# Re-ordering the first loads, the bound chain and the plan of layer 1's first stage in a two-layer linear-attention / gated-MLP kernel

## The chip, the cores and the metric

The kernel runs on one core of a Trainium2 chip. The metric is the device time of one launch in microseconds (us), the median of several runs. In what follows PE is the matrix engine, DVE the vector engine, ACT the scalar engine, POOL the GpSimd engine, and SP the engine that issues most DMA transfers; ACT issues a few of its own.

## The reference, cut to what matters

Four residual steps on `x` of 2048 tokens by 576, in bf16: attention A, MLP B, attention A, MLP B, all with the same weights.

```python
def A(x):                                  # 32 heads of 18
    q, k, v = split(layernorm(x) @ wqkv)   # wqkv: 576 x 1728
    pq, pk = q @ w_phi, k @ w_phi          # w_phi: per head 18 x 18
    phi_q = concat(softmax(pq), softmax(-pq))
    phi_k = concat(softmax(pk), softmax(-pk))
    kv, z = phi_k.T @ v, phi_k.sum(over tokens)
    return (phi_q @ kv) / (phi_q @ z + 1e-6) @ wo
def B(x):
    n = layernorm(x)
    return ((n @ w_gate) * (n @ w_up)) @ w_down     # 576 -> 4608 -> 576
x = x + A(x); x = x + B(x); x = x + A(x); x = x + B(x)
```

`kv` and `z` sum over all tokens, so no token of a layer gets its attention output before the key side of all tokens is done. This is the barrier of each layer.

## The kernel before, in words

The 2048 tokens are 16 tiles of 128 tokens, in 8 pairs ("blocks"). The model width of 576 is cut into five slices of 128 rows, the last one holding 64 rows twice. `w_phi` is multiplied into the query and key weights at the start, so that `x @ Wk` gives `pk` at once: `t_fuse1` (L1003) takes one row block of the raw weights (`Wraw`, five blocks), transposes its five 128-column pieces on PE (L1012), copies them from PSUM to `WT` (L1015), multiplies by a block-diagonal `w_phi` (`BDphi`, L879 and L1025), and copies the result into `Wk` or `Wq` (L1031).

The program has two versions of everything behind a branch: softmax without the subtraction of a maximum ("fast"), taken if a bound shows that no exponent can overflow, and a general one. The bound is worked out by `t_flag` (L883). It needs the largest entry of `w_phi` (L888), the diagonal blocks of `Wraw`'s Gram matrix, summed over all five row blocks (L893, fifty 128x128 matmuls), the row maxima of these on DVE (L896), a transposition of three columns on PE in f32 (L901), and four small DVE steps in a row (L907 to L910), the last of which writes the flag. Each engine loads the flag and branches (L248, L249). What stands ahead of the branch in each engine's program is the shared part. In these runs the fast version is taken.

The first stage after the branch is layer 1's key side. For each tile, layer norm (`t_ln`, L1042) does bn_stats twice (L1066), an aggregate (L1074), the reciprocal root on ACT (L1087, L1089), and the normalised tile `xln` on POOL or DVE (L1099, a piece of 576 columns, and a repeat of 64 for tiles that a DMA transposes). The tile is transposed by PE (L1107, L1110) for the first four tiles and by a DMA (L1114) for the rest. `t_v` (L1346) projects values (PE L1140, ACT copies L1370). `t_ain` with `fast_front` projects keys (PE L1140, four ACT exponentials L1261), and `softmax_tail` sums (DVE L1327), inverts (ACT L1334, or DVE L1330) and multiplies (L1342: POOL, or DVE for the last two tiles). `kv_ops` accumulates `kv` in two PSUM banks (PE L1381). Key tiles use six buffers, which come free when `kv_ops` has read them. A projection here is 18 matmuls on row halves of 64.

`t_qproj` (L1271) projects queries of tiles 2 to 15 and stores them in place of the tile (PE L1140, ACT L1284). `t_aout` (L1475) turns a tile's queries into its attention output. For tiles 0 and 1 of layer 1 it does so by PE transposes (L1493), and only after the barrier (`t_barrier`, the masked copy `BD`, L1466) come the numerator (L1523), its division (L1531 to L1545), the output projection (L1557, L1578, L1128) and the second layer norm. Then the MLP of block 0 starts (`gu_quad`, PE L1662). From there on, MLP blocks (gate and up L1662, down L1736 and L1738) run back to back, with the attention work of later tiles laid between their matmuls.

Nothing of this order is written by hand. Each `t_` function is a thread of a planner (`Sched`, L295 on), which at build time estimates when each operation could start and appends the earliest to its engine's program, corrected by priorities, by per-thread constants in `AGES` (L19), and by per-operation costs. Each engine then runs its list in order, waiting on semaphores. So a change in a cost, a priority or an age moves instructions throughout; on the chip an instruction that waits holds up all that stand behind it on its engine.

The loads at the start (`t_load`, L915): SP issues tile 0 of x, raw block 0, raw block 2, tile 1, raw block 4 (64 rows, loaded twice into the two partition halves), the value weights `Wv` in three transfers, and tiles 2 to 7 in three. ACT issues `w_phi` in two, raw block 1 and raw block 3.

## Time and profile before

| what | value |
|---|---|
| median of 6 runs | 1078.48 us (1077.53 to 1079.17) |
| the profiled execution's own time | 1078.44 us |
| its span in the trace | 1076.7 us |
| PE busy | 1053.4 us, 98% |
| DVE, ACT, POOL busy | 483.7, 346.1, 202.2 us |
| first bound matmul (L893) | 4.20 us |
| flag written (end of L910) | 19.14 us |
| first sum of exponentials (L1327) | 27.40 us |
| `BD` done (L1466) | 84.50 us |
| first matmul of the MLP (L1662) | 101.32 us |

Times in the trace count from the start of the span. The span is 1.74 us shorter than the execution's time, which lies around it. "PE busy" counts a matmul from its start to its modelled end, so PE that waits a little inside a group still counts as busy.

### The profile page before, as it was taken

The page shows a single profiled execution, that of the slowest core. Times are in us where ns is not written, and L with a number is a line of the kernel's source. Part 1 is how long each engine was busy: PE and PEld are TensorE (multiplying, and loading weights), DVE is VectorE, ACT ScalarE, POOL GpSimd, SP SyncE. Part 2 cuts the span into 40 slices and gives each one's busy share as a digit, 9 for nine tenths or more (in the row PEclk, how much of TensorE's full clock was granted, in tenths as well). Part 3 has the DMA queues.
Part 4 walks back from the last instruction along what each step waited for, and adds up shares of the span by engine and source line. Part 5 has one row for each costly group of instructions (what it writes and reads, how often), then busy time and mean ns, then how long its engine had stood idle before and what let it go on. Part 6 is the DMA issues. An engine that isn't in the chain of part 4 may idle for free.

```text
span 1076.7 us, 34366 instructions
## 1 busy us (share of the span) xinstructions
PE 1053.4 (98%) x15812; PEld 806.9 (75%) x15812; DVE 483.7 (45%) x974; ACT 346.1 (32%) x838; POOL 202.2 (19%) x232
## 2 busy tenths in 40 slices
PE   6999999999999999999999999999999999999997
PEld 5667868778686878878685787777778686868683
DVE  5986436344443535425332754434434243424131
ACT  4777224314241422314140642231313131302120
POOL 2764004022130403103020030201010101000000
PEclk9999999999999999999999999999999999999999
DMA  4486264260916335181605134536271809080604
GB/s 134 113 271 239 38 187 85 71 177 14 225 35 194 65 113 140 38 194 37 199 14 166 35 58 113 146 87 171 63 196 39 220 19 239 15 222 16 210 2 146
DMA packets 177642, 127.79 MB, mean 119 GB/s; under 512 B 96592, under 2 KB 175696, under 8 KB 176336
## 3 DMA queue, kind: packets, MB, share of 16 engines
q1 hardware_dynamic: 176592, 124.85, 44.5%
q8 instruction: 126, 2.06, 0.8%
q10 hardware_dynamic: 896, 0.64, 0.2%
q14 instruction: 28, 0.23, 0.1%
HBM read 100.82 MB, written 2.36 MB: 96 GB/s over the span
## 4 chain that ended last, share of the span: by engine, by line
PE 92%; DMA 2%; POOL 2%; DVE 2%; ACT 1%; issue 0%; ACTq 0%
PE ps L1662 53%; PE ps L1736 22%; PE ps L1140 11%; PE ps L1738 3%; PE ps L1523 1%; DMA wdx<-in_B_w_down_dram 1%; POOL dd_w3f L1342 1%; PE ps L1381 1%; PE ps L1128 1%; DMA Wraw<-in_A_wqkv_dram 1%; DVE xln L1099 1%; POOL dd_h1g L1342 1%; DVE ss_w4f L1327 0%; DMA wdr<-in_B_w_down_dram 0%; PE ps L1107 0%; PE ps L893 0%
## 5 line engine op out<-in xcount | busy, mean ns | idle before, releaser
L1662 PE MATMUL ps<-xT,Wg 64*128 64x256 bf16 x4608 | 582.3, 269 | 0.0
L1662 PE MATMUL ps<-xT,Wu 64*128 64x256 bf16 x4608 | 582.0, 269 | 0.0
L1662 PEld LDWEIGHTS ps<-xT,Wu 64*128 64x128 bf16 x4608 | 432.1, 94 | 27.4 <-DVE x_sb L1777 0.3
L1662 PEld LDWEIGHTS ps<-xT,Wg 64*128 64x128 bf16 x4608 | 430.7, 94 | 28.8 <-issue 3.1
L1711 DVE TENSOR_TENSOR hT<-ps,hT 128x512 bf16<-128x512 f32 x288 | 199.2, 692 | 299.8 <-ACT hT L1709 299.8
L1709 ACT CAST hT<-ps 128x512 bf16<-128x512 f32 x288 | 168.4, 585 | 412.2 <-PE ps L1662 402.2
L1736 PE MATMUL ps<-wdr,hT 128*128 128x512 bf16 x960 | 244.2, 380 | 1.3 <-DMA wdr<-in_B_w_down_dram 1.3
L1342 POOL TENSOR_TENSOR dd<-dd,ss 128x576 bf16<-128x576 bf16 x92 | 107.5, 1194 | 415.4 <-ACT ss L1338 415.4
L1738 PE MATMUL ps<-wdr,hT 128*128 128x64 bf16 x960 | 185.1, 193 | 0.0
L1736 PEld LDWEIGHTS ps<-wdr,hT 128*128 128x128 bf16 x960 | 93.8, 98 | 112.4 <-DMA wdr<-in_B_w_down_dram 1.9
L1662 PE MATMUL ps<-xT,Wr 64*128 64x256 bf16 x1152 | 170.4, 269 | 0.0
L1099 POOL TENSOR_SCALAR xln<-x_sb,nmean,rstd 128x64 bf16<-128x64 bf16 (+1 forms) x94 | 58.2, 625 | 340.1 <-DVE nmean L1080 157.9
L1779 DVE TENSOR_TENSOR x_sb<-ps,x_sb 128x64 bf16<-128x64 f32 x32 | 7.1, 221 | 224.8 <-PE ps L1738 224.8
L1738 PEld LDWEIGHTS ps<-wdr,hT 128*128 128x128 bf16 x960 | 94.1, 98 | 0.2
L1338 ACT ACTIVATE ss<-ss 128x64 f32<-128x64 f32 x92 | 23.6, 258 | 175.8 <-DVE ss L1327 175.0
L1327 DVE TENSOR_REDUCE ss<-dd 128x64 f32<-128x1152 bf16 x48 | 63.8, 1348 | 21.1 <-ACT dd L1261 16.1
L1662 PEld LDWEIGHTS ps<-xT,Wr 64*128 64x128 bf16 x1152 | 66.8, 94 | 6.2
L1736 PE MATMUL ps<-wdx,hT 128*128 128x512 bf16 x192 | 54.3, 380 | 1.2 <-DMA wdx<-in_B_w_down_dram 1.1
L1140 PE MATMUL ps<-Wk,xT 64*128 64x288 bf16 x576 | 49.9, 286 | 2.3 <-ACT vx_w0g L1370 1.4
L1140 PE MATMUL ps<-Wv,xT 64*128 64x288 bf16 x576 | 49.1, 288 | 0.0
L1066 DVE BATCH_NORM_STATS2 st<-x_sb 128x6 f32<-128x288 bf16 x120 | 46.3, 445 | 2.3 <-DMA x_sb<-in_A_x_dram 1.5
L1140 PE MATMUL ps<-Wo,oT 64*128 64x288 bf16 x504 | 40.5, 283 | 0.0
(120 smaller groups left out, 741.4 us busy)
## 6 DMA issues: line engine op xcount, KB each, us to landing
wdr<-in_B_w_down_dram SPq DMA_DIRECT2D x240, 288.0 KB, 3.6
wdx<-in_B_w_down_dram SPq DMA_DIRECT2D x48, 288.0 KB, 3.7
Wg<-in_B_w_gate_dram SPq DMA_DIRECT2D x4, 1152.0 KB, 14.9
Wu<-in_B_w_up_dram SPq DMA_DIRECT2D x4, 1152.0 KB, 16.9
out_dram<-x_sb SPq DMA_DIRECT2D x16, 144.0 KB, 2.3
x_sb<-in_A_x_dram SPq DMA_DIRECT2D x7, 288.0 KB, 5.3
xT<-xln SPq DMA_TRANSPOSE x54, 2.6
Wraw<-in_A_wqkv_dram SPq DMA_DIRECT2D x2, 304.0 KB, 4.1
```

The source lines that it names most:

```text
L1066: ops.append(Op(d_dve(288), (lambda e, j=j, h=h, src=src: e.bn_stats(st[:, sl[j], 6 * h:6 * h + 6], src)), reads=rd, writes=[("st", sl[j], ...
L1099: em = [(lambda e, j=j, a=a, b=b, c=c: e.tensor_scalar(xln[:, sl[j], a:b], x_sb[:, ss[j], c:c + b - a], s.nmean[:, sl[j]:sl[j] + 1], rstd[ ...
L1128: full = [Op(d_pe(N), (lambda e, k=k, h=h: e.matmul(s.ps[:, banks[h], 0:N], L[:, k, :], Wm[:, k, N * h:N * h + N], start=(k == 0 and fresh ...
L1140: out.append(Op(61, (lambda e, h=h, k=k, st=(i == 0 and k == 0), sp=(i == 1 and k == 3): e.matmul(s.ps[:, banks[h], 0:N], L[r, k, :], Wm[r ...
L1327: Op(1265, (lambda e: e.tensor_reduce(ss[:, sm, :], e4, AX.X, ALU.add)), reads=s.ddk(sm, 0) + s.ddk(sm, 1), writes=[("ss", sm)]),
L1338: yield ("ops", "act", [Op(200, (lambda e, kw=kw: e.activation(ss[:, sm, :], ss[:, sm, :], **kw)), reads=[("ss", sm)], writes=[("ss", sm)])])
L1342: yield ("alt", [(eng, [Op(dur, (lambda e, ev=ev, rb=rb: e.tensor_tensor(ev, ev, rb, ALU.mult)), reads=s.ddk(sm, br) + [("ss", sm)], write ...
L1662: out.append(Op(54.3, (lambda e, bank=bank, cs=cs, lhsT=lhsT, rhs=rhs, st=st, sp=sp: e.matmul(ps[:, bank, cs].rearrange("p (a n) -> p a n" ...
L1709: yield ("ops", "act", [Op(480, (lambda e, gb=gb, p=p: e.copy(hT[:, p, :], ps[:, gb, :])), reads=[("gu", gb)], writes=[("hT", p)] + (s.raw ...
L1711: yield ("ops", "dve", [Op(600, (lambda e, ub=ub, p=p: e.tensor_tensor(hT[:, p, :], ps[:, ub, :], hT[:, p, :], ALU.mult)), reads=[("gu", u ...
L1736: ops = [Op(d_pe(512), (lambda e: e.matmul(s.ps[:, bank, 0:512], lhsT, s.wslot(slot)[:, fi, 0:512], start=(f == 0), stop=(f == NF - 1))), ...
L1738: Op(d_pe(64) + 3, (lambda e: e.matmul(s.ps[:, z, 64 * sl:64 * sl + 64], lhsT, s.wslot(slot)[:, fi, 512:576], start=(f == 0 and (sl == 0 o ...
```

## The change

It has these parts.

1. Loads. Raw block 4 is one transfer of 128 rows (448 to 575) instead of 64 rows twice. SP now issues tile 0, raw 0, tile 1, raw 2, raw 3, raw 4, `Wv`, and tiles 6 to 9; ACT issues `w_phi`, raw 1, tiles 2 and 3, and tiles 4 and 5 (`sload`, `aload`). For raw block 4 the fused product uses only the second 64 columns of the transposed piece and writes 64 partitions.
2. The bound. A new thread `t_m2` brings the square of `w_phi`'s maximum onto all partitions early, by two small f32 matmuls. Behind the last Gram matmul there remain the two row maxima, one comparison per partition, two matmuls with a vector of ones that count the partitions, and one comparison with 255.5.
3. The order around the branch. Layer 1's thread has priority 12 and takes its two `kv` banks only after the branch; the planner's own estimate of the wait at the branch is 750 instead of 500 ns. As built, the 18 value matmuls of tile 0, and on DVE the bn_stats of tiles 2, 3 and half of those of tile 4, stand ahead of the branch; `BDphi` is made on POOL and tile 0's `xln` on DVE.
4. The rest. The planner's costs of `xln` on POOL are 790 and 370 ns instead of 620 and 200. Query copies of layer 1 may go to DVE too (`qalt`). `qlead` is 12 instead of 8, so the query side of tiles 0 and 1 may start after key tile 4 instead of 8. The `kv` matmuls no longer have to come in tile order (`kv_fresh`). `AGES` is replaced as a whole. The option to transpose the raw weights by DMA (`wtdma`) is present but empty, so this is not used.

As built, PE's fast program ahead of the first MLP matmul holds 252 row-half query matmuls (before: 190 and 20 of full height), and behind it 26 fewer query matmuls than before. The order of the MLP part is otherwise nearly the one of before.

```diff
@@ planner settings
+        self.wtdma = ''
+        self.valt = False
+        self.qalt = True
+        self.sload = [['x0', 0], ['raw', 0], ['x0', 1], ['raw', 2], ['raw', 3], ['raw', 4], ['wv', 0], ['x', 3]]
+        self.aload = [['raw', 1], ['x', 1], ['x', 2]]
+        self.rord = (0, 1, 2, 3, 4)
-        self.qlead = 8 if fast else 8
+        self.qlead = 12 if fast else 8
-        self.fqp = 6.15 if fast else 6.5
+        self.fqp = 6.5 if fast else 6.5
-                            t_ = self.tr.fin[tr.lastw[r[1]]] + 500.0
+                            t_ = self.tr.fin[tr.lastw[r[1]]] + 750.0
@@ the bound
+    def t_m2(self):
...
+        (_, bank), = yield ("acqn", ["pb"], 1)
+        row, col = s.ps[0:1, bank, 0:128], s.ps[:, bank, 128:129]
+        yield ("ops", "pe", [... e.matmul(row, s.cst[:, 0:1], s.identf[:], start=True, stop=True, ...)])
+        yield ("ops", "dve", [... e.tensor_reduce(s.flg[0:1, 0:1], row, AX.X, ALU.max) ...,
+                              ... e.tensor_scalar(s.flg[0:1, 1:2], s.flg[0:1, 0:1], s.flg[0:1, 0:1], None, ALU.mult) ...])
+        yield ("ops", "pe", [... e.matmul(col, s.onesf[0:1, :], s.flg[0:1, 1:2], start=True, stop=True, ...)])
+        yield ("ops", "dve", [... e.tensor_copy(s.cst[:, 3:4], col) ...])
@@ t_flag, behind the two row maxima
-        yield ("ops", "pe", [Op(150, (lambda e, c=c: e.matmul(s.ps[0:1, bank, 128 * c:128 * c + 128], s.cst[:, c:c + 1], s.identf[:], ...)) for c in range(3)])
-            Op(470, ... e.tensor_reduce(s.flg[0:1, 0:3], ...)
-            Op(70, ... e.tensor_tensor(s.flg[0:1, 3:4], ...)
-            Op(70, ... e.tensor_scalar(s.flg[0:1, 4:5], ...)
-            Op(70, ... e.tensor_scalar(s.flag[0:1, 0:1], s.flg[0:1, 4:5], lim, None, ALU.is_lt))
+        yield ("ops", "dve", [... e.tensor_scalar(s.f01[:], s.cst[:, 1:3], s.cst[:, 3:4], lim, ALU.mult, ALU.is_lt) ...])
+        yield ("ops", "pe", [... e.matmul(n01, s.f01[:, c:c + 1], s.one16[:], start=(c == 0), stop=(c == 1), ...) for c in range(2)])
+        yield ("ops", "dve", [... e.tensor_scalar(s.flag[0:1, 0:1], n01, 255.5, None, ALU.is_gt) ...])
@@ t_load
-            for p, queue in zip(range(0, 128, n), queues):
-                yield ("dma", g, ... e.dma_start(s.Wraw[p:p + n, kt, :], wqkv[128 * kt:128 * kt + n, 0:2 * D + 64]) ...)
+            r0 = 128 * kt if kt < 4 else D - 128
+            em = lambda e: e.dma_start(s.Wraw[:, kt, :], wqkv[r0:r0 + 128, 0:2 * D + 64])
@@ t_fuse1
-                        s.ps[:, bank, c:c1], WT[:, kt, k, :], s.BDphi5[:, k, a:b, :], ...
+                        s.ps[r, bank, c:c1], WT[:, kt, k, 0 if kt < 4 else 64:], s.BDphi5[:, k, a:b, :], ...
@@ t_ln, planner costs of xln
-                           for eng, dur in (("pool", (620, 200)[:2 - fast]), ("dve", (400,) if fast else (400, 200)))[:1 + (fast or boot)]])
+                           for eng, dur in (("pool", (790, 370)[:2 - fast]), ("dve", (400,) if fast else (400, 215)))[:1 + (fast or boot)]])
@@ kv_ops and t_layer1
-                start=st, stop=last, skip_group_check=True)),
+                start=s.kv_fresh(bi) if first is None else st, stop=last, skip_group_check=True)),
-        gots = yield ("acqn", ["pb"], 2)
-        s.kvb = [g_[1] for g_ in gots]
         yield ("wait", "init")
...
         yield ("wait", "branch")
+        gots = yield ("acqn", ["pb"], 2)
+        s.kvb = [g_[1] for g_ in gots]
@@ build
+        sc.launch(self.t_m2(), 9, "m2")
-        sc.launch(self.t_layer1(), 5, "A1")
+        sc.launch(self.t_layer1(), 12, "A1")
```

## The prediction

> **What bounds the kernel now.** I read the page's busy shares first: PE is busy for 1053.4 of 1076.7 us, so the search is for the 23.3 us in which it isn't, and for stretches where it is slow. Next I read busy time by stretch over the span.
>
> ```profile
> 4.00:6.00 2.00, 1.78 (x15) 1.52 (x15) 1.42 (x4) 0.50 (x2) 1.10 (x1) 1.00 0.92 308
> 6.00:8.00 2.00, 0.00 (x0) 0.00 (x0) 0.49 (x1) 0.00 (x0) 0.47 (x1) 1.00 1.02 311
> 8.00:10.00 2.00, 0.94 (x10) 0.95 (x11) 0.19 (x1) 0.00 (x0) 0.00 (x0) 1.00 1.07 244
> ...
> 18.00:20.00 2.00, 0.20 (x4) 0.06 (x2) 1.18 (x5) 0.18 (x1) 0.18 (x1) 1.00 0.00 0
> ...
> 22.00:24.00 2.00, 2.00 (x20) 1.27 (x18) 1.43 (x9) 1.71 (x7) 0.00 (x0) 0.50 0.00 0
> ...
> 40.00:45.00 5.00, 4.50 (x74) 3.60 (x74) 5.00 (x14) 3.39 (x13) 4.90 (x6) 1.00 0.14 44
> ...
> 85.00:90.00 5.00, 5.00 (x82) 3.47 (x77) 3.38 (x9) 4.14 (x9) 0.00 (x0) 1.00 1.00 412
> ...
> 101.30:200.00 98.70, 98.70 (x1603) 80.32 (x1599) 46.51 (x94) 33.25 (x79) 23.41 (x26) 1.00 0.40 88
> ```
>
> Columns: stretch, length, PE, PEld, DVE, ACT, POOL busy, clock, DMA share, GB/s. PE has nothing at 6 to 8 us while DMA is full, and next to nothing at 18 to 20, around the branch; then it runs at half clock. At 40 to 45 DVE and POOL are full and PE is not. From 85 on PE is full, and stays so from the MLP on; only 8 us of idle lie behind 1000 us, where the change does nothing. So the change can act on the first 101 us, and behind that only through how much PE work is left. Then the chain of waits up to the MLP:
>
> ```profile
> 1.89 7.12 DMA Wraw<-in_A_wqkv_dram
> ...
> 15.52 0.56 PE ps L893 x10
> ...
> 19.00 0.15 DVE flag L910
> 19.15 0.81 issue
> ...
> 21.51 4.52 PE ps L1140 x44
> ...
> 27.40 1.35 DVE ss_w4f L1327
> ...
> 36.99 4.61 POOL dd_h1g L1342 x4
> ...
> 64.30 4.62 POOL dd_w3f L1342 x4
> 68.97 0.69 PE ps L1381 x13
> ...
> 99.01 2.31 PE ps L1140 x36
> ```
>
> It runs over a raw block's landing (9.01 us), PE's bound matmuls, the flag's DVE steps, 0.81 us at the branch, then over DVE and POOL, and over PE in the last 16 us. Last, the timeline, for what DVE does behind the branch:
>
> ```profile
> 19.85 2.98 DVE L1066 BATCH_NORM_STATS2 st<-x_sb 128x6 f32<-128x288 bf16 x8 [0.71 <-DVE flag L910]
> 23.89 2.14 DVE L1099 TENSOR_SCALAR xln<-x_sb,nmean,rstd 128x576 bf16<-128x576 bf16 x5 [0.54 <-ACT rstd L1089]
> 27.40 1.35 DVE L1327 TENSOR_REDUCE ss_w4f<-dd_h1g 128x64 f32<-128x1152 bf16 x1 [1.37 <-ACT dd_h1g L1261]
> ```
>
> The first sum of exponentials starts 7.55 us after DVE is back from the branch.
>
> **What the Trainium skill says.** "TensorE: Matmul & The Clock Gate", Part 1: PE starts at half clock, gets the full clock after some 3.4 us of activity and loses it after an idle window. The trace agrees: ten bound matmuls take 1.27 us at 9.56 and 0.72 at 15.37, and the clock is 0.50 at 22 to 24. "DMA: Bandwidth & Descriptors", section "Issuing engines are not separate DMA queues": moving loads from SP to ACT saves issue time, not bandwidth. The trace agrees: at 4.2 to 5 us SP's and ACT's queues moved 0.12 MB each, together 307 GB/s. Same page, "Rules for kernel authors": two partition halves are best one transfer; the halves of raw 4 landed 6.1 and 7.0 us after issue. "Advanced Engine Details and Errata", "Mode Summary": DVE's second port is shared with GpSimd. The trace agrees: an `xln` of 576 took DVE 0.43 us at 15.22 and 1.04 at 34.04, beside POOL's multiplies.
>
> **Part by part.** The profiled execution took 1078.44 us, 1.74 more than its span and 0.04 below the median; I count against it.
>
> *A, up to the branch.* Between raw 1's landing and the end of the last bound matmul, PE has the same work in both programs (40 bound matmuls, 15 transposes, 15 fused products, 6 tile transposes: 9.06 to 16.09). So raw blocks first helps only as far as raw 1 lands sooner. Raw 1 keeps its place behind `w_phi` on ACT's queue, but no raw 3 shares it. Bounds: 0, and all of PE's wait, -3.1. I take -0.7, because the slowest transfer, not the mean, ends the wait, and the bytes ahead of it hardly change. The chain behind: before, 3.06 us (16.09 to 19.15). After: two row maxima 0.89, a `WT` copy that stands between 0.49, the comparison 0.15, then two bn_stats at 0.37 that stand ahead of the flag's last step and cover PE's tiny matmuls, 0.74, the step 0.15, latencies 0.15: 2.57, so -0.5. Four bn_stats (1.5 us) precede the row maxima; PE covers them with twenty bound matmuls, but at full clock these are 1.1 to 1.4 us: +0.6 of order. Sum -0.6. `t_m2`'s two f32 matmuls (0.27 each, from six in 0.82) and its DVE steps lie in the wait for raw 1; uncovered they cost some 1 us. `BDphi` on POOL: 1.19 us (L1342) times 720/576 is 1.5, ready near 6.4, needed after 9. ACT's two added DMA issues (0.47 each) fall where ACT idles for 7.1 us; SP's transfers of tiles 6 to 9 stand behind `Wv`. The single transfer of raw 4 and the 64-partition products cost nothing: same bytes, same columns. Taking the two `kv` banks after the branch frees two PSUM banks ahead of it, where PE waits for data and not for banks: 0. The branch itself stays 0.81; the planner's 750 ns only moves its plan.
>
> *B, from the branch to the first sum.* Before 7.55. After, on DVE: a `Wk` copy 0.40, two bn_stats 0.74, aggregates 0.41, `nmean` 0.17, wait for ACT 0.54, six `xln` at 0.43, 2.6: 4.9. On ACT: two value copies 0.72, `WTq` 0.69, `Wk` 0.40, layer-norm steps 1.2, `Wq` 0.41, four exponentials 1.35: 4.8. Both end at 4.9, so -2.6. PE's half clock, if it comes again, hides: some 23 products and transposes and 28 projections stand ahead, about 2.2 us, 4.4 at half clock.
>
> *C, first sum to `BD`.* Before 57.1 us, with DVE idle for 5.7. DVE's work from here on: one reciprocal (0.55) and two weight copies (0.9) fewer, two `xln` pairs more (0.8 to 1.6 each), net +0.3. POOL loses three `xln` pairs' worth, 3 x 0.82 + 2 x 0.43 = 3.3 us. But the end is built differently. Before, DVE's own multiply fed the last `kv` matmuls, and `BD` followed 1.45 us later. After, a sum and a reciprocal are followed by two multiplies on POOL (2.4), `kv` (0.9), `BD` (1.4): 4.8, so +3.3. Against this stands POOL's relief in a stage whose chain lies on POOL from 37 to 49 and 63 to 69; I take half, -1.6. Net +2.0; the new ages shift what stands where by amounts that I can't sum one by one, so I keep wide bounds: -1.0 (the relief also frees key buffers sooner, and DVE's idle time halves) and +8.7 (below).
>
> *D, `kv` end to MLP.* Before 17.5 us (83.8 to 101.3). After, the phi_q of tiles 0 and 1 is transposed before the barrier, and the numerator needs only `BD`: it starts 1.45 behind `kv` instead of 2.35. In PE order: 8 q, numerator, 28 q, numerator, then the second tile's chain to its `Tx`, near 13.5, and 44 q behind, 2.7: 16.2. So -1.3 (bounds -2.0 and +0.5). Four query copies (0.40 each) move from ACT to DVE here; DVE waits 2 us for the numerator in this stretch, which covers them, and without that cover they cost 1.6.
>
> *E, the rest.* 26 fewer query matmuls at 0.064 (2.31/36): -1.7, since PE is full there. The work goes ahead of `kv`'s end, where PE has slack. Value tile 0 before the branch (18 matmuls, 1.2 us) is hidden likewise.
>
> Sum: -0.6 - 2.6 + 2.0 - 1.3 - 1.7 = -4.2; 1078.44 - 4.2 = 1074.2.
>
> **The rivals.** *The relief carries through* (C = -1.0): -7.2, 1071.2. For it: the chain's POOL pieces; against it: DVE is full from 30 to 60 regardless. *The lead is lost in line* (A = 0, C = +3.6, no relief): -2.0, 1076.4. For it: raw 1 may land at 9.0 again, and value tile 0 waits in PE's list for `Wv`, ahead of the flag's two matmuls; `Wv` landed at 13.2 before, and 0.6 MB more stand ahead of it now, 2 us at 300 GB/s, so 15.2, against some 15.9 when it is needed. *Slower: work for after the barrier goes ahead of it.* With `qlead` 12 the softmax of tiles 0 and 1 on the query side stands in front of the last key tiles: two sums on DVE (2.7) and four multiplies on POOL (4 x 1.42 = 5.7). If all 8.4 lie on the way to the last `kv`, C is 8.7, and the sum is +2.5: 1080.9. It decides once POOL has no idle time between 65 us and the barrier; before, POOL's 75 to 80 was a third busy, which speaks against the full price.
>
> **How the numbers follow.** A measurement can tell about 0.2%, 2.2 us, from no change. Forecast 1074.2 (own range 1072.0 to 1076.5): 0.50. Relief, 1071.2: 0.20. Lead lost, 1076.4, straddling the limit: 0.18. Slower, 1080.9: 0.12. Faster: 0.46 + 0.20 + 0.06 = 0.72. Same: 0.04 + 0.12 + 0.02 = 0.18. Slower: 0.10. The range 1070.0 to 1078.8 leaves out the far ends of the first and the last rival.
>
> **What would show it.** A: L910's successor ends near 18.5 instead of 19.14. B: the first sum starts near 24.2 instead of 27.4. C: `BD` is done near 83.3. D: the MLP starts near 98.8. E: from there to the end, 1.7 us less. It is wrong if the raw blocks land before 7 us (then A is larger), if PE waits for `Wv` ahead of the branch, or if POOL runs without a gap into the last `kv`.

## The result, and the profile after

| | before | after |
|---|---|---|
| median | 1076.79 us (71 runs, 1072.62 to 1079.17) | 1076.08 us (34 runs, 1074.32 to 1079.32) |
| ratio after/before, 95% interval | | 0.9994 (0.9989 to 1.0000) |
| the profiled execution, own time / span | 1078.44 / 1076.7 us | 1078.01 / 1076.3 us |

The change makes no difference that this measurement can tell: 0.7 us between the medians, where 4.2 were forecast. The time lies in the forecast's range, but the sum that led to it is wrong in one term. Milestones show which. In this table and in all that follow, a stage runs from the end of one milestone to the next: the flag written, the start of the first sum of exponentials, `BD` done, the first MLP matmul in the timeline, the end of the span.

| stage, us | before | after | difference | forecast |
|---|---|---|---|---|
| start to flag | 19.14 | 18.16 | -1.0 | A -0.6 |
| flag to first sum | 8.26 | 5.34 | -2.9 | B -2.6 |
| first sum to `BD` | 57.10 | 65.10 | +8.0 | C +2.0 |
| `BD` to MLP | 16.66 | 14.88 | -1.8 | D -1.3 |
| MLP to end | 975.54 | 972.82 | -2.7 | E -1.7 |
| sum | 1076.7 | 1076.3 | -0.4 | -4.2 |

Four of five terms came a little better than forecast, 8.4 us together, and one took nearly all of it back. (The first MLP matmul of before is at 101.16 us in the timeline; the table ahead of the prediction had its group at 101.32.) The lines that answer to those of before follow; first the busy time by stretch of the changed kernel, columns as there.

```profile
4.00:6.00 2.00, 1.59 (x12) 1.07 (x12) 0.91 (x4) 0.50 (x2) 0.59 (x1) 1.00 0.82 267
6.00:8.00 2.00, 1.23 (x11) 0.67 (x10) 1.41 (x4) 0.00 (x0) 0.80 (x1) 1.00 1.01 361
8.00:10.00 2.00, 2.00 (x17) 1.79 (x16) 1.52 (x5) 0.98 (x2) 0.00 (x0) 1.00 1.06 392
18.00:20.00 2.00, 1.59 (x25) 1.00 (x22) 1.22 (x5) 1.21 (x4) 0.88 (x4) 1.00 0.00 0
22.00:24.00 2.00, 2.00 (x29) 1.24 (x27) 1.64 (x5) 1.86 (x6) 0.00 (x0) 1.00 0.37 86
40.00:45.00 5.00, 5.00 (x80) 4.31 (x81) 4.83 (x7) 3.99 (x15) 4.08 (x5) 1.00 0.72 64
60.00:65.00 5.00, 4.17 (x37) 2.37 (x39) 3.92 (x4) 3.29 (x11) 3.92 (x4) 0.66 1.09 179
```

PE works where it had nothing before, at 6 to 8 and 18 to 20 us, and has its full clock at 22 to 24 instead of half. POOL at 40 to 45 is no longer full. A new weak spot is at 60 to 65: PE at clock 0.66, and no engine full. Next the chain of waits up to the MLP.

```profile
1.31 4.03 DMA wst<-in_A_w_phi_dram
5.52 1.45 DVE xln L1144
...
15.06 0.67 PE ps L931 x10
...
18.49 0.41 issue
...
24.96 1.23 ACT dd_h1g L1306 x4
...
61.13 4.28 PE ps L1185 x37
65.41 1.32 ACT dd L1306 x4
...
71.36 1.36 DVE ss_w4f L1373
...
73.29 2.42 ACT dd_w3f L1306 x8
...
76.09 1.29 ACT eT L1551 x2
...
82.87 4.23 PE ps L1185 x64
...
100.84 2.80 PE ps L1185 x44
```

The chain begins with the second transfer of `w_phi` (`wst`) instead of a raw block, and with an `xln` of 1.45 us; the parts of the start come back to both. The POOL pieces of 4.6 us that stood in it before are gone; from the branch to the MLP no POOL piece is left. In their place, from 61 to 77 us, stand projections (L1185, 37 matmuls, most of them the queries'), query exponentials (`dd`, L1306) and copies of transposed query weights (`eT`, L1551): work whose result is used behind the barrier, in the chain that leads up to it. Last, DVE in the timeline, first behind the branch, then in the last part of the stage.

```profile
18.03 0.13 DVE L944 TENSOR_SCALAR flag<-ps 1x1 int32<-1x1 f32 x1
...
18.94 0.46 DVE L1076 CAST Wk<-ps 128x288 bf16<-128x288 f32 x1 [0.78 <-PE ps L1185]
...
23.50 1.35 DVE L1373 TENSOR_REDUCE ss_w4f<-dd_h1g 128x64 f32<-128x1152 bf16 x1 [0.32 <-ACT dd_h1g L1306]
...
62.61 1.34 DVE L1373 TENSOR_REDUCE ss_w4f<-dd_w3f 128x64 f32<-128x1152 bf16 x1
67.36 2.61 DVE L1373 TENSOR_REDUCE ss<-dd 128x64 f32<-128x1152 bf16 x2 [3.40 <-ACT dd L1306]
71.36 1.35 DVE L1373 TENSOR_REDUCE ss_w4f<-dd_h1g 128x64 f32<-128x1152 bf16 x1 [1.39 <-ACT dd_h1g L1306]
74.83 1.35 DVE L1373 TENSOR_REDUCE ss_w4f<-dd_w3f 128x64 f32<-128x1152 bf16 x1 [2.11 <-ACT dd_w3f L1306]
...
81.46 1.35 DVE L1373 TENSOR_REDUCE ss_w4f<-dd_h1g 128x64 f32<-128x1152 bf16 x1
```

The first sum starts at 23.50 us, 3.9 before that of the old kernel. `ss_w4f` is a key tile, `ss` a query tile. Sixteen key sums have to be done before `BD`; counted off in both timelines, the twelfth starts at 64.5 us before and at 62.6 after, so 1.9 us of the lead is left. The thirteenth starts at 67.9 before and at 71.4 after: the lead is gone, and 3.5 us more. Between the two, DVE does two query sums (2.61 us) and stands idle 3.40 and 1.39 us.

### The profile page after: what moved, and what is told of

Its sections match the earlier page's. It is cut to its first block, busy times and chain, and to the rows that moved or that the text cites. A ratio compares the mean times of both kernels' runs of the same rounds, so it can differ in the third digit from the quotient of the medians.

```text
span 1076.3 us, 34402 instructions
## 1 busy us (share of the span) xinstructions
PE 1057.0 (98%) x15828; PEld 806.8 (75%) x15828; DVE 484.2 (45%) x982; ACT 346.7 (32%) x839; POOL 196.3 (18%) x226
## 4 chain that ended last, share of the span: by engine, by line
PE 94%; DVE 2%; DMA 2%; ACT 2%; issue 0%
PE ps L1715 53%; PE ps L1789 22%; PE ps L1185 12%; PE ps L1791 3%; PE ps L1575 1%; DMA wdr<-in_B_w_down_dram 1%; PE ps L1427 1%; DVE ss_w4f L1373 1%; DVE xln L1144 1%; ACT dd_h1g L1306 1%; PE ps L1152 0%; PE ps L1173 0%; DMA wdx<-in_B_w_down_dram 0%; ACT dd_w3f L1306 0%; DMA wst<-in_A_w_phi_dram 0%; PE ps L931 0%
## 5 line engine op out<-in xcount | busy, mean ns | idle before, releaser
L1144 POOL TENSOR_SCALAR xln<-x_sb,nmean,rstd 128x576 bf16<-128x576 bf16 x86 | 51.7, 607 | 254.4 <-DVE nmean L1125 173.6
L1185 PE MATMUL ps<-Wk,xT 64*128 64x288 bf16 x576 | 49.5, 285 | 2.8 <-ACT Wq L1076 1.7
L1185 PE MATMUL ps<-Wv,xT 64*128 64x288 bf16 x576 | 49.7, 283 | 1.6 <-ACT eT L1551 0.5
L1185 PE MATMUL ps<-Wq,xT 64*128 64x288 bf16 x576 | 42.4, 289 | 0.1
```

What stands on the lines that cost most here:

```text
L1144: em = [(lambda e, j=j, a=a, b=b, c=c: e.tensor_scalar(xln[:, sl[j], a:b], x_sb[:, ss[j], c:c + b - a], s.nmean[:, sl[j]:sl[j] + 1], rstd[ ...
L1185: out.append(Op(61, (lambda e, h=h, k=k, st=(i == 0 and k == 0), sp=(i == 1 and k == 3): e.matmul(s.ps[:, banks[h], 0:N], L[r, k, :], Wm[r ...
```

## The experiments

The planner decides the order, so one setting can't be changed without everything moving. Most experiments therefore *replay* an order: the planner's choice behind the branch is taken from a list of steps (thread, step, engine), which was recorded from the plan of before or of after and then edited. The edit, the same in each of them:

```diff
@@ Sched.run, behind the branch
+            if self.script and hasattr(self, "mark_time"):
+                best = self.follow() or best
             _, th, est = best
@@ build
+    fast.sc.script = [... ORDER ...]
```

All milestones first. Ratios are against the kernel before, with 95% intervals; the other columns come from one profile each.

| kernel | flag | to first sum | to `BD` | to MLP | to end | ratio |
|---|---|---|---|---|---|---|
| before | 19.14 | 8.26 | 57.10 | 16.66 | 975.54 | |
| after | 18.16 | 5.34 | 65.10 | 14.88 | 972.82 | 0.9994 (0.9989 to 1.0000) |
| start_only | 17.40 | 6.12 | 57.11 | 16.66 | 973.81 | 0.9972 (0.9959 to 0.9985) |
| order_only | 18.43 | 8.06 | 64.13 | 14.89 | 972.79 | 1.0023 (1.0013 to 1.0033) |
| start | 16.78 | 6.01 | 61.60 | 16.66 | 974.35 | 0.9986 (0.9970 to 1.0002) |
| late_old | 17.65 | 5.35 | 59.09 | 16.67 | 975.74 | 0.9994 (0.9984 to 1.0004) |
| early_old | 17.25 | 6.13 | 66.82 | 14.89 | 973.21 | 1.0024 (1.0016 to 1.0032) |
| k12_up | 19.02 | 5.33 | 64.49 | 15.46 | 971.70 | 0.9996 (0.9985 to 1.0006) |
| q_late | 17.65 | 5.33 | 73.37 | 14.88 | 973.87 | 1.0059 (1.0043 to 1.0076) |
| k1213_up | 17.90 | 5.34 | 67.49 | 15.45 | 973.32 | 1.0049 (1.0033 to 1.0064) |
| q_early | 18.08 | 6.69 | 60.52 | 15.63 | 975.88 | 1.0006 (0.9994 to 1.0019) |
| old_loads | 19.23 | 5.89 | 57.11 | 16.66 | 975.31 | 0.9981 (0.9973 to 0.9989) |
| old_bound | 17.19 | 6.12 | 58.59 | 16.66 | 974.64 | 0.9980 (0.9971 to 0.9988) |
| late_old_l7 | 17.98 | 5.33 | 62.10 | 17.04 | 973.95 | 1.0028 (1.0016 to 1.0039) |

### The start alone, the order alone, and the start with the planner's old settings

*start_only* is the changed kernel up to the branch (loads, bound chain, shared part) with the order of before behind it. *order_only* is the reverse. *start* has no replay: the changed kernel, with the old settings for the plan.

```diff
# start_only: after, with
+ORDER = """... recorded from before, behind the branch ..."""
# order_only: before, with
-        self.qlead = 8 if fast else 8
+        self.qlead = 12 if fast else 8
+ORDER = """... recorded from after, behind the branch ..."""
# start: after, with AGES and the costs of xln of before, and
-        self.qalt = True
+        self.qalt = False
-        self.qlead = 12 if fast else 8
+        self.qlead = 8 if fast else 8
-        self.fqp = 6.5 if fast else 6.5
+        self.fqp = 6.15 if fast else 6.5
```

(order_only also takes over `kv_fresh` and the choice of DVE for query copies, without which the new order can't be followed.)

> The changed kernel up to the branch (new loads, new bound chain, shared value tile), but behind the branch every engine takes its steps in the order of the kernel before. Theory 1 (the gain of the start is lost in the new order from key tile 12 on, where the query side of tiles 0 and 1 stands ahead of key tiles 12 to 15): flag near 18.2 us, BD about 3 us sooner than before's 84.5, near 81.5, MLP near 98.3, the rest unchanged at 975.4; in all 3 us less than before, a ratio near 0.997. Theory 2 (the stage is bound by DVE and POOL and takes up any earlier start, whatever the order): BD at 84 to 84.5, ratio 0.999 to 1.000.

> The kernel before up to the branch (old loads, old bound chain), but behind the branch every engine takes its steps in the order of the changed kernel. Theory 1: the first sum a little sooner than before (26 to 27 us, since part of the shorter way to it lies in the order), BD near 91 to 92, MLP near 106, the rest 972.7 as in the changed kernel; in all about 3 us more than before, ratio 1.003. Theory 2: BD at 88 to 89 as in the changed kernel, MLP near 103.7, ratio 0.999 to 1.000.

> Part 4 of the change undone, the planner making its own order: the old ages, the old costs of the normalised tile on POOL and DVE, the old query lead (8), query copies on ACT alone, the old priority of the query weights; loads, bound chain and shared part as in the changed kernel. Theory 1 (the old settings still fit the new start): first sum near 23.5 us, from there to BD 57 to 58 us, BD near 81, ratio 0.997. Rival (ages belong to one exact start, and with another start the plan falls apart): from the first sum to BD 60 us or more, ratio 0.999 or more.

The two halves part cleanly. With the new start and the old order the stage to `BD` is as long as before (57.11 against 57.10), the MLP starts 3.9 us sooner (97.29 against 101.16), and the kernel is 0.28% faster. With the old start and the new order it is 64.13, the MLP starts 4.35 us later (105.51), of which 2.75 come back behind it, and the kernel is slower. So the start is a gain, and the order costs more than it brings. *start* makes of the old settings another order, with a stage of 61.60 in its profile, 4.5 more than the order recorded from before. That this order is worse isn't shown: its timed ratio overlaps start_only's, and PE's clock is 0.50 to 0.91 at 52 to 56 and at 68 to 74 us of this profile.

### Which part of the order

*late_old* follows after's order up to the first projections of key tile 12 and that of before from there on; *early_old* is the reverse, cut at key tile 11.

```diff
# late_old
-ORDER = """... after to K12a ... after to the end ..."""
+ORDER = """... after to K12a ... before to the end ..."""
# early_old
+ORDER = """... before to K11 ... after to the end ..."""
```

> The changed kernel, with its own order as far as the first projections of key tile 12 (11 of the 16 sums of exponentials), and from there on the order of the kernel before. Theory 1: the twelfth sum near 62.6 us as in the changed kernel, the thirteenth near 66 instead of 71.4, BD near 81.5, MLP near 98, the rest near 975.4 (the 26 query matmuls are behind the MLP's start again); ratio 0.997. Theory 3 (the new order loses evenly over the stage, or already ahead of tile 12): BD at 86 or later, ratio 0.999 to 1.000.

> The changed kernel, with the order of the kernel before as far as the projections of key tile 11, and from there on the changed kernel's own order. Theory 1: the gap between the twelfth and the thirteenth sum is 8 us or more, as in the changed kernel (8.8), BD at 88 to 90; ratio 0.999 to 1.001. Theory 3: half or more of the loss is gone, BD at 85 to 86, ratio 0.998 or less.

Put onto the old order, the early part alone adds 2.0 us to the stage (59.09 against 57.11), the late part alone 9.7 (66.82). Put onto each other, the late part adds 6.0 (65.10 against 59.09), the early part takes 1.7 off (65.10 against 66.82). So they don't add up, but the late part is the large one either way, and the last four key tiles are where to look. Written as PE's list (K a key tile's projections with halves a and b, V values, KV the sums over tokens, A0 and A1 the query projections of tiles 0 and 1, T their transposes, Q later queries):

```
before: ... K12 V12 K13 KV11 K14 K15 KV9 A0 A1 V13 V14 V15 KV13 Q3 Q2 T0 KV15 T1 Q4 Q5
after:  ... K12a A0a A1a A0b A1b K12b V12 K13a KV11 K13b KV11 KV9 K14 K15 T0 T1 V13a V14 V15 Q2 KV15 Q3 Q4 V13b Q5 Q6 KV13
```

DVE's list in after has the sums of A1, A0, K13, K15, K14 and only then K12, and POOL's multiplies of A1 and A0 stand ahead of those of K13 and K12. The timelines of after show what that does, first PE, then ACT, then POOL.

```profile
60.82 1.52 PE L1185 MATMUL ps<-Wk,xT 64*128 64x288 bf16 x10 [1.73 <-ACT Wq L1076]
61.90 3.95 PE L1185 MATMUL ps<-Wq,xT 64*128 64x288 bf16 x36
65.57 0.77 PE L1185 MATMUL ps<-Wk,xT 64*128 64x288 bf16 x8
```

```profile
65.40 2.53 ACT L1306 ACTIVATE dd<-ps 128x288 bf16<-128x288 f32 x8 [0.87 <-PE ps L1185]
67.73 0.50 ACT L1306 ACTIVATE dd_h1g<-ps 128x288 bf16<-128x288 f32 x1
...
77.63 0.56 ACT L1306 ACTIVATE dd_h1g<-ps 128x288 bf16<-128x288 f32 x1
```

```profile
69.56 4.61 POOL L1388 TENSOR_TENSOR dd<-dd,ss 128x576 bf16<-128x576 bf16 x4 [1.49 <-ACT ss L1384]
83.47 2.33 POOL L1388 TENSOR_TENSOR dd_h1g<-dd_h1g,ss_w4f 128x576 bf16<-128x576 bf16 x2 [7.01 <-DVE ss_w4f L1376]
```

All 36 query projections (`Wq`) stand between the two halves of key tile 12's (`Wk`), then eight query exponentials ahead of the first of tile 12's four (67.73). Its last one, at 77.63, comes behind those of tiles 13 to 15 and four copies of transposed query weights. On POOL four query multiplies stand ahead of tile 12's. POOL is not short of time: it idles 7.01 us before the multiplies of tile 12, the last ones of the stage. In start_only the same sums come without the gap:

```profile
60.57 1.35 DVE L1783 TENSOR_REDUCE ss_w4f<-dd_w3f 128x64 f32<-128x1152 bf16 x1 [0.23 <-ACT dd_w3f L1716]
...
64.04 1.35 DVE L1783 TENSOR_REDUCE ss_w4f<-dd_h1g 128x64 f32<-128x1152 bf16 x1 [1.42 <-ACT dd_h1g L1716]
...
69.08 1.35 DVE L1783 TENSOR_REDUCE ss_w4f<-dd_w3f 128x64 f32<-128x1152 bf16 x1 [1.81 <-ACT dd_w3f L1716]
...
72.40 1.35 DVE L1783 TENSOR_REDUCE ss<-dd 128x64 f32<-128x1152 bf16 x1
```

These are the twelfth, the thirteenth and the fifteenth key sum; the first query sum (`ss`) comes behind them, and no idle time is longer than 1.81 us.

### Repairing the late part of after, a piece at a time

If one misplaced piece is the cause, moving it alone repairs the stage. *k12_up* moves tile 12 and values 13 forward; *q_late* moves the query projections behind key tile 15 and leaves tile 12's last exponential and its sum late; *k1213_up* moves tiles 12 and 13 both ahead of the query side.

```diff
# PE's list, with ACT's, DVE's and POOL's to match
-... K12a A0a A1a A0b A1b K12b V12 K13a KV11 K13b KV11 KV9 K14 K15 T0 T1 V13a V14 V15 Q2 KV15 ... V13b ... KV13
+k12_up:   ... K12a K12b A0a V12 A0b A1a A1b K13a KV11 K13b KV11 KV9 K14 K15 T0 T1 V13 V14 V15 Q2 KV13 KV15
+q_late:   ... K12 V12 K13a KV11 K13b KV11 KV9 K14 K15 A0 A1 V13a V14 V15 ... V13b T0 T1 Q5 Q6 KV13
+k1213_up: ... K12 K13 V12 A0 A1 KV11 KV9 K14 K15 T0 T1 V13 V14 V15 Q2 KV13 KV15
```

> The changed kernel in its own order, except that the steps of key tile 12 and of the value tiles 12 and 13 stand where their tile numbers put them, ahead of the query side of tiles 0 and 1; this query side still stands ahead of key tiles 13 to 15. Theory 1a (the query side in front of the last key tiles costs most of the 6 us that the new late order loses): the next sums still come late, BD at 86.5 or later, ratio 0.998 to 1.000. Theory 1b (key tile 12 and value tile 13, left behind until the very end, are the cause): BD near 83.5, 5 us sooner than the changed kernel's 88.6, ratio 0.995 to 0.997.

> The changed kernel in its own order, except that the query side of tiles 0 and 1 (36 projections, 8 exponentials, 2 sums, 4 multiplies, 18 transposes, 4 copies) stands behind the projections of key tile 15; key tile 12 and value tile 13 stay as late as in the changed kernel. Theory 1a: the thirteenth sum near 66 us instead of 71.4, BD near 84, ratio 0.996 to 0.998. Theory 1b: the thirteenth sum comes sooner, but tile 12 still ends the stage: BD at 87 or later, ratio 0.999 or more.

> The changed kernel in its own order, except that the steps of the key and value tiles 12 and 13 stand ahead of the query side of tiles 0 and 1 and of the kv matmuls of tiles 8 to 11; the query side still stands ahead of key tiles 14 and 15. Theory 1c (two things stand in the way of tiles 12 and 13, the query side and those kv matmuls, which wait for POOL; either one alone leaves a gap of 7 us; behind tiles 12 and 13 the query side is nearly free, since tiles 14 and 15 have to wait for buffers until some 66 us anyway): no gap over 4.5 us between the sums of the last five key tiles, BD at 83 to 84, MLP near 98.5 to 99, ratio 0.996 to 0.997. Theory 1a (the query side ahead of any key tile costs its whole length): BD at 86.5 or later, ratio 0.999 or more.

None repairs it: 64.49, 73.37 and 67.49. Each has a gap of 7 to 8 us between two key sums, only at another place: 66.6 to 73.5 us in k12_up, 61.1 to 68.2 in q_late, 66.4 to 74.5 in k1213_up. The timelines of q_late and k1213_up say why.

```profile
65.52 0.35 PE L1837 MATMUL ps<-vx_w0g,dd_w3f 128*128 128x76 bf16 x5 [2.10 <-POOL dd_w3f L1798]
65.80 0.99 PE L1595 MATMUL ps<-Wk,xT 64*128 64x288 bf16 x8
...
68.21 1.35 DVE L1783 TENSOR_REDUCE ss_w4f<-dd_h1g 128x64 f32<-128x1152 bf16 x1 [5.73 <-ACT dd_h1g L1716]
```

```profile
72.88 4.61 POOL L1796 TENSOR_TENSOR dd<-dd,ss 128x576 bf16<-128x576 bf16 x4
...
77.54 2.10 PE L1953 MATMUL ps<-ident,dd 128*128 128x128 bf16 x18 [4.91 <-POOL dd L1796]
```

In q_late the query side is out of the way, and the gap is there all the same: PE waits 2.10 us for a multiply of POOL's, at a `kv` group of earlier tiles (L1837), with K13b right behind it; tile 13's exponentials and sum come late, and DVE idles 5.73 us. In k1213_up both key tiles are early. Its gap holds the two query sums (2.61 us on DVE) and two waits of 2.1 us for ACT's exponentials; behind it PE waits 4.91 us at the query transposes for POOL's four query multiplies, with V13 to V15 behind, which `kv` needs. (The 73.37 of q_late is on the high side: its profiled run is the slowest of its four, 3.0 us above their median, with half clock at 66 to 70 and at 82 to 90 us.) So the theory that tile 12 and 13 being late is the whole cause fell, and so did the one that the query projections on PE are. What the runs have in common, as far as these lines show, is the form: a step that waits for another engine, with steps behind it in the same list that could have gone and that the barrier needs.

*q_early* asks the reverse: the good order of start_only, with the query side of tiles 0 and 1 alone put early.

```diff
# start_only's list
-K13 KV11 K14 K15 KV9 A0 A1 V13 ... T0 ... T1
+K13 A0 A1 KV11 K14 K15 KV9 T0 T1 V13 ...      (exponentials ahead of K13's, sums and multiplies ahead of K13's)
```

> start_only (order of the kernel before behind the branch) with one thing of the changed order: the query side of tiles 0 and 1 stands behind the projections of key tile 13, on ACT and DVE ahead of tile 13's exponentials and sum, on POOL ahead of its multiplies, and its transposes ahead of the value tiles 13 to 15. Theory 1 (the query side alone is enough): BD 4 to 7 us later than start_only's 80.63, at 85 to 87.5, ratio 1.000 or more. Rival (it needs the late tile 12 and the kv matmuls in the way as well): BD at 81 to 82.5, ratio 0.998 or less.

The stage grows by 3.4 us (60.52 against 57.11) and the ratio from 0.9972 to 1.0006, intervals apart. So the query side ahead of the last key tiles costs by itself a little under half of the 8.0. In PE's timeline it waits again at the transposes, 1.47 us at the first tile's and 1.61 at the second's:

```profile
76.59 0.68 PE L1953 MATMUL ps<-ident,dd 128*128 128x128 bf16 x9 [1.61 <-POOL dd L1796]
```

### The early part

The early order puts more of the `xln` on DVE. *late_old_l7* is late_old with the four `xln` instructions of tiles 14 and 15 on POOL.

```diff
-lnA1_7:5:dve lnA1_7:6:dve
+lnA1_7:5:pool lnA1_7:6:pool
```

> As late_old (the changed kernel's order to key tile 12, then that of before), but the normalised tiles 14 and 15 are made on POOL, as before the change, and not on DVE; POOL idles for 5.25 us at that time. Theory P (the changed order loses 2 us ahead of tile 12 because these four instructions, 3.2 us, stand on DVE ahead of the sum of key tile 11): the twelfth sum near 59.5 us instead of 62.1, BD near 80 instead of 82.1. Rival: POOL's 2.5 us ahead of the multiplies of tiles 9 and 10 delay the kv matmuls that free key buffers, and BD stays at 82.

```profile
56.77 2.62 POOL L1552 TENSOR_SCALAR xln<-x_sb,nmean,rstd 128x576 bf16<-128x576 bf16 x4 [2.89 <-ACT rstd L1542]
...
61.12 1.35 DVE L1781 TENSOR_REDUCE ss_w4f<-dd_w3f 128x64 f32<-128x1152 bf16 x1 [2.65 <-ACT dd_w3f L1714]
```

DVE is spared 3.17 us of `xln`, and the twelfth sum comes 1.0 us sooner (61.1 against 62.1). But the sums of tiles 13 to 15 start within 0.2 us of late_old's, the last one 2.3 us later, and the stage is 62.10, 3.0 longer; the timed ratio is worse too. So the theory that `xln` on DVE costs the early part's 2.0 us found no support. The profile can't refute it cleanly, for PE's clock is 0.50 to 0.67 at 60 to 64 and at 70 to 74 us here and 1.00 throughout in late_old; the projections of tile 12 and its values alone took 1.5 us longer. No other run settles the 2.0 us.

### The parts of the start

*old_loads* is start_only with the old order of the loads (raw 4 still in one transfer), *old_bound* start_only with the old bound chain, without `t_m2`.

```diff
# old_loads
-        self.sload = [['x0', 0], ['raw', 0], ['x0', 1], ['raw', 2], ['raw', 3], ['raw', 4], ['wv', 0], ['x', 3]]
-        self.aload = [['raw', 1], ['x', 1], ['x', 2]]
+        self.sload = [['x0', 0], ['raw', 0], ['raw', 2], ['x0', 1], ['raw', 4], ['wv', 0], ['x', 1], ['x', 2]]
+        self.aload = [['raw', 1], ['raw', 3]]
# old_bound
-    def t_m2(self):
...
-        sc.launch(self.t_m2(), 9, "m2")
+    def t_flag(self):      (as before: three f32 matmuls and four DVE steps behind the row maxima)
```

> As start_only (start of the changed kernel, order of the kernel before behind the branch), but the loads in the order of before: SP issues tile 0, raw 0, raw 2, tile 1, raw 4 (one transfer), Wv, tiles 2 to 5; ACT issues w_phi, raw 1, raw 3. If the loads bring the sooner flag: flag at 18.3 to 19, 1 us later than start_only's 17.4. If the bound chain brings it: flag at 17.4 to 17.8 still. From the flag to the first sum 6.1 in both cases.

> As start_only, but the bound worked out as in the kernel before: three transpositions in f32 on PE, then four small DVE steps in a row. By the prediction's working the chain behind the last bound matmul is then 0.5 us longer: flag at 17.9 to 18.1. If the short chain is worth more than its own length because it also lets work stand ahead of the branch, the first sum is later by over 1 us (24.6 or later, 23.5 in start_only).

With the old loads the flag is at 19.23 us, as before; with the new ones and the old chain it is at 17.19, not later than with both (17.40). This does not put the sooner flag down to the order of the loads. Raw 1 lands at 9.01 us in before and at 9.18 in order_only, but between 6.92 and 7.99 in the twelve others, and old_loads, with its old order, is one of them (7.72). What the twelve share and the two lack is, among other things, raw 4 in one transfer; no run changes that alone. Nor does PE in after wait for raw 1 there. In the nine kernels with after's shared part the second group of bound matmuls starts 4.13 to 4.15 us after the second transfer of `w_phi` has landed (4.96 to 5.83 us), wherever raw 1 is. Between the two stand DVE's maximum, tile 0's `xln` and this tile's transposes. In old_loads `w_phi` landed at 5.88, and the planner also laid out the shared part anew, with that group behind ten transposes at 10.55; so its late flag is no price of the loads.

In the timed ratio the two kernels are 0.1% behind start_only, with overlapping intervals: neither part is shown to matter by itself. Most of what start_only gains is behind the flag, and is there without the new loads too: to the first sum 5.89 us in old_loads, 8.26 before. The timelines of PE, after and then old_bound, show why the flag is no sooner with the short chain.

```profile
5.66 0.59 PE L914 MATMUL ps<-identf,cst 128*1 128x128 f32 x2 [0.33 <-DVE cst L911]
7.02 0.85 PE L1152 MATMUL ps<-ident,xln 128*128 128x128 bf16 x6 [0.77 <-DVE xln L1144]
...
8.45 0.58 PE L917 MATMUL ps<-flg,onesf 1*128 1x1 f32 x2
9.47 1.27 PE L931 MATMUL ps<-Wraw 128*128 128x128 bf16 x10
```

```profile
5.80 0.85 PE L1549 MATMUL ps<-ident,xln 128*128 128x128 bf16 x6 [0.31 <-DVE xln L1541]
...
8.12 1.27 PE L1325 MATMUL ps<-Wraw 128*128 128x128 bf16 x10
```

The chain behind the last bound matmul did get shorter: 15.72 to 18.16 us in after, 2.44; 13.69 to 17.19 in old_bound, 3.50. But the second bound group starts at 9.47 instead of 8.12, and the last one ends 2.0 us later: the 1.1 us gained at the end are lost at the front. Two things stand at the front in after. One is `t_m2`, with two f32 matmuls (0.59 and 0.58 us with what follows each). The other is an `xln` of 1.45 us, beside which POOL makes `BDphi`; in old_bound `BDphi` is on DVE and the `xln` takes 0.42. *start*, whose own plan keeps `BDphi` on DVE, parts them: it has `t_m2` as well, its `w_phi` landed later (5.63 against 5.34), and its second bound group starts at 8.53, with the soonest flag of all. First POOL in after, then DVE in start:

```profile
5.41 1.39 POOL L901 TENSOR_TENSOR BDphi<-wst,mask 128x720 bf16<-128x720 bf16 x1 [1.50 <-DMA wst<-in_A_w_phi_dram]
```

```profile
5.82 0.42 DVE L1142 TENSOR_SCALAR xln<-x_sb,nmean,rstd 128x576 bf16<-128x576 bf16 x1
```

So the move of `BDphi` to POOL, more than `t_m2`, seems to have eaten what the short chain gained. No run makes this move alone.

All flags are single profiles. They lie between 17.25 and 19.02 us in the nine kernels with one and the same shared part, so a difference of 1 us between two of them says little; the reading of the chain rests on the waits and starts in these lines, not on the flag.

## Why the prediction was right or wrong, point by point

**A, up to the branch: right within the scatter.** -1.0 for a forecast of -0.6, but its pieces were sized wrongly and cancel, which is luck. The landing was to start the second bound group 0.7 us sooner; it starts at 9.47 instead of 9.56, -0.1. From there to the end of the last bound matmul it is -0.3 (6.53 to 6.25), where +0.6 of order was forecast. The chain is 3.05 before and 2.44 after, -0.6 for -0.5. Raw 1 did land 1.45 us sooner, but PE now waited for the steps that lead from `w_phi` to the transposes of `xln`. So the sentence fails that `t_m2`'s matmuls "lie in the wait for raw 1": there was no wait left to hide them. And "`BDphi` on POOL: ... ready near 6.4, needed after 9" left out what it stands beside: it was ready at 6.80 and in time, and the `xln` on DVE took 1.45 us. "PE waits for `Wv` ahead of the branch" did not happen; 18 to 20 us is filled with that very work.

**B, to the first sum: right.** DVE is back at 18.94 and starts the first sum at 23.50, 4.56 us; forecast 4.9, before 7.55. A part of this was not in the forecast's sum, which took the half clock for hidden. In before PE's 44 projections at 21.51 stand on the chain, 4.52 us, mostly at half clock, and DVE idles 1.37 us for them; at the 0.064 us each of later ones they would take 2.8. So up to 1.7 us of B may be PE's clock (an estimate), which is 1.00 at 22 to 24 in every profile with the new start. Of the 2.9 us between flag and sum, 2.1 belong to the start (start_only, 6.12) and 0.8 to the order.

**C, first sum to `BD`: the failed term, "net +2.0", measured +8.0.** The forecast took the stage for a sum of busy time: DVE +0.3, a longer end +3.3, and "against this stands POOL's relief in a stage whose chain lies on POOL ...; I take half, -1.6". The relief is real, 3.3 us in this stage (POOL is busy for 38.5 us instead of 41.8), and POOL left the chain; the stage isn't shorter for it. Two things stand in its place. The first is PE, which the sum leaves out: the prediction says that the moved query work goes "ahead of `kv`'s end, where PE has slack". The stage in before, then in after, columns as above:

```profile
27.40:84.50 57.10, 53.06 (x790) 37.55 (x788) 51.62 (x83) 44.12 (x150) 41.81 (x38) 1.00 0.72 209
23.50:88.60 65.10, 59.94 (x852) 40.62 (x849) 52.28 (x84) 49.05 (x161) 38.45 (x34) 0.97 0.74 216
```

PE had 4.0 us of slack before. It is busy 6.9 us longer after, and idle 1.1 longer. ACT, too, has 4.9 us more. The query work that was added is some 2.7 us (an estimate: 42 row halves more, a matmul of full height counted as two, at 0.064); it comes back in D and E. The rest of the 6.9 is lower clock and waits inside groups, which count as busy. The second thing is the order in the lists. Nearly all of the 8.0 is in the late part of the order, which costs 6.0 us onto the new early part and 9.7 onto the old one. The query side put early costs 3.4 when it is alone (q_early), where PE is busy only 0.9 us longer and idle 2.3 longer, so most of that is waits. In after, tile 12's sum and multiplies last of all, values 13 late, and `kv` groups that wait for POOL ahead of K13b come on top. I can't give each a price, nor part the added work from the waits: taking one away leaves a gap of the same size at the next one. That the new order costs 7 to 8 under either start (64.13 with the old one, where before has 57.10; 65.10 with the new one, where start_only has 57.11) makes it the order and not its meeting with the new start.

Part of C is neither. PE's 36 query matmuls take 3.95 us in after, at clock 0.66, and 2.38 in order_only, at 1.00:

```profile
65.29 2.38 PE L1552 MATMUL ps<-Wq,xT 64*128 64x288 bf16 x35 [0.37 <-ACT dd_w3f L1673]
```

This is about 1.0 to 1.6 us, and the stage lengths 65.10 and 64.13 differ by 1.0. The same scatter separates start_only and old_bound, which have one order behind the branch, and stages of 57.11 and 58.59; PE in the timeline, start_only first:

```profile
58.50 0.65 PE L1595 MATMUL ps<-Wk,xT 64*128 64x288 bf16 x8
```

```profile
58.56 1.17 PE L1582 MATMUL ps<-Wk,xT 64*128 64x288 bf16 x8
```

The same eight matmuls, at half the speed in old_bound, whose clock is 0.75 from 56 to 60 us, against 1.00.

So a stage in one profile is known to about 1.5 us. That the clock is scatter alone isn't shown: somewhere between 58 and 90 us PE has half clock in five of the six profiles with after's late list and in three of the eight others, so a part of it may be the order's. The 6.0, the 8.0 and the 9.7 stand clear of that; the 2.0 and the 1.7 of the early part barely.

**D, `BD` to MLP: right.** -1.8 for -1.3, and it is the order's: 14.88 to 15.46 us in the six kernels that end with after's list, 16.66 to 17.04 in those that end with before's; q_early, a cross of the two, has 15.63.

**E, the rest: right.** -2.7 in this pair; over the profiles, 975.0 on average in the seven with before's list there and 972.95 in the six with after's, -2.0 for a forecast of -1.7. Single profiles scatter by 1 to 2 us; part of that is PE's waits for `w_down`, 2.4 us in before, 1.1 in after, 0.5 in start_only.

**The rivals.** *Relief carries through* (1071.2) is refuted: the relief came and the stage grew. *Lead lost in line* (1076.4) has nearly the measured time and the wrong reason: A came in full, and `Wv` was in time. *Work for after the barrier goes ahead of it* named the mechanism and a price, C = +8.7, close to the +8.0; but it summed the price on DVE and POOL, and the time was lost on PE and in waits, so that the two figures are close is luck. It didn't end slower than before because A, B, D and E together brought 8.4 where I had given 6.2. I gave it 0.12 for the reason that "it decides once POOL has no idle time between 65 us and the barrier": this test is wrong. POOL had idle time in plenty (7.01 us in one piece), and the price was paid all the same, since in a list that runs in order a step can be late while the engine that it needs is idle.

**What stays open.** How much of C is the added work on PE and how much the waits. The cause of the early part's 2.0 us, and why it turns to -1.7 in front of the late part of after. The share of each misplaced step in the late part. Whether a plan exists that has D and E (-3.8) without the price in C; of the five late orders tried (after, k12_up, q_late, k1213_up, q_early), none does. The best of all kernels here is start_only, the new start with the old order: 1073.99 us, 0.9972 (0.9959 to 0.9985), faster than before; after's interval lies above its own. Part of such small differences goes with PE's clock: 151 timed runs of the kernel before average 1078.9 us where the run's mean clock was 0.995 and 1075.9 where it was 0.999, and start_only's mean was 0.9983 against 0.9968; whether the clock is the cause there isn't shown.

## What to carry to other kernels

In a stage with a barrier at its end, cost a re-ordering by the step that each waiting instruction holds up in its own engine's list, and not by the busy time of the engine that seems to bound the stage alone; add up the moved work on every engine, PE too. The gaps between the sixteen sums showed in one view where the time went. Work for behind a barrier is free ahead of it only if nothing that the barrier needs stands behind it in any of the lists it passes, and an engine with idle time is no proof of that. A gain at the start and a new plan should be measured apart: here one brought 3.0 us, and the other took 2.4 of them.

## What the runs showed of the hardware that was not expected

PE lost its full clock behind short waits, and not each time. The Trainium skill ("TensorE: Matmul & The Clock Gate", Part 1) gives an idle window of some 3.4 us for that. Here a wait of 1.73 us for the copy of `Wq` comes with a clock of 0.66 over 60 to 65 us in after, while late_old kept 1.00 behind a like wait (1.74 us). One and the same wait of 1.38 us, in lists that are equal there, left 1.00 in start_only and 0.75 in old_bound. The page's remark that the window runs freely, so that the same kernel differs from run to run, would fit this; no run here shows the window.

An `xln` of 576 columns took DVE 1.45 us at 5.52 (the chain of after), where the prediction has 0.43 for one without company; POOL made `BDphi` from 5.41 to 6.80. It is 1.44 to 1.45 us in all ten profiles in which `BDphi` is made on POOL, and 0.42 to 0.43 in the four in which it is on DVE. The skill ("Advanced Engine Details and Errata", "Mode Summary") has it that DVE's second port is shared with GpSimd; the trace agrees and gives the price, a factor of three, in a place where PE waits for this `xln` (0.77 us, at 7.02).
